# Attention decoding: the first part of the first keys in two loads of 64 partitions each instead of one of 128

## The chip, the cores and the metric

The kernel runs on one core of a Trainium2 chip. The metric is the device time of one execution in microseconds, the median of the runs. A profile of one execution, taken by the hardware profiler, is read beside it; its span goes from the first to the last instruction and is a little shorter than the measured time.

## What is computed

Attention for one query position against 65,536 keys, with 32 query heads that share 8 key and value heads (four to one). All tensors are bfloat16; D is 128.

```python
B, Hq, Hkv, Sq, Sk, D = 1, 32, 8, 1, 65536, 128
...
k = jnp.repeat(k, rep, axis=1)
v = jnp.repeat(v, rep, axis=1)
scale = D ** -0.5
scores = jnp.einsum("bhqd,bhkd->bhqk", q, k) * scale
p = _softmax(scores, axis=-1)
return jnp.einsum("bhqk,bhkd->bhqd", p, v)
```

The keys and the values are 134.2 MB each, and each byte is read from HBM once.

## The kernel before

**Tiling.** A head's 65,536 keys are taken in two rounds of 32,768 (`NR` is 16 rounds in all for the 8 heads, `HALVES` is 2). In a round each of the 128 partitions holds 2T = 256 consecutive keys of 128 numbers: 64 KB in a row, 8.39 MB over all partitions. A "row tile" is one key of each partition, 128 x 128 numbers. The keys of a round lie in `kbuf`, which has room for 256 + 96 row tiles, so that rounds alternate between two overlapping places; the values lie in `vbuf`, 256 row tiles.

**A round.** TensorE transposes the key tiles in groups of TB = 8 into one of four PSUM buffers (`pe_transposes`, line 139); VectorE and ScalarE copy them to `ktb` in SBUF (`evict`, lines 233 and 235); TensorE multiplies each with the four queries of the head (`pe_scores`, line 157), LAG = 8 groups behind the transposes. The maximum over a part of the scores is taken on VectorE and GpSimd, the exponentials on ScalarE (line 403), and TensorE multiplies them with the values (`stretch`, line 183). A round is cut into 160 and 96 row tiles (A and C), each with its own maximum.

**Loads.** All loads of keys and values are issued by SyncE (SP) in `sync_engine`, in the order in which they stand there, on one queue. A key load waits for `kfree`, which ScalarE raises (line 231) when the first 160 row tiles of the round before are transposed; a value load waits for `vfree`. From the second head on, each round is one load of keys and one of values of 8.39 MB. The loads of the first head and of the last rounds are cut into parts, so that work can start sooner at the beginning and little is left to do at the end. The keys of round 0 come in three parts, at `K_PARTS` = (0, 64, 160): 64, 96 and 96 row tiles of all 128 partitions, or 2048, 3072 and 3072 KB. They go to the columns C to C + 256 of `kbuf`.

**Semaphores.** Each part of the keys has one, `krdy[0]` to `krdy[2]`. A load adds 16 to it when it has landed. TensorE waits for `krdy[n]` and takes the 16 away again (`take`, lines 42 to 45) ahead of the group of transposes that needs the part: `krdy[0]` before group 0, `krdy[1]` before group 8, and `krdy[2]` before group 19. Such waits stand in the profile under line 45, the line of `take`.

**The start.** TensorE waits for the queries and an identity matrix, transposes the queries (line 215), waits for their copy (`t_qT`) and enters the loop over the rounds, whose beginning is aligned with up to 16 empty instructions. The first thing in the loop is the wait for `krdy[0]`.

Of the kernel before, what the change touches and what calls it, by code (L numbers as in the profile page):

```python
# [10 lines left out]
P = 128  # L11
# [3 lines left out]
C = 96  # L15
A = 2 * T - C
K_PARTS = (0, 64, A)
# [24 lines left out]
def take(e, sem, n=1):  # L42

    e.wait_ge(sem, n)
    e.sem_inc(sem, -n)  # L45


def bass_standalone__gqa_softmax__decode_kernel(nc, q, k, v, out):
# [14 lines left out]
    def row_tile(odd, x):  # L63
        return (x + C) % (2 * T) if odd else x
# [6 lines left out]
    def sb(name, shape, dt):  # L71
        return S(nc.sbuf_tensor(name, shape, dt))

    def sem(name):
        return S(nc.semaphore(name))

    kbuf = sb("kbuf", [P, (2 * T + C) * D], DT.bfloat16)
# [38 lines left out]
    krdy = [sem(f"krdy{i}") for i in range(len(K_PARTS))]  # L116
    vrdy = [sem(f"vrdy{i}") for i in range(2)]
    vpiece = [sem(f"vpiece{i}") for i in range(len(V_PIECES))]
    kfree, vfree, vmid = sem("kfree"), sem("vfree"), sem("vmid")
    trd, tra, evd, eva = sem("trd"), sem("tra"), sem("evd"), sem("eva")  # L120
    qkd, qrdy, pvd = sem("qkd"), sem("qrdy"), sem("pvd")
# [42 lines left out]
    def pe_keys(pe, i):  # L164
        for j in range(GA + LAG):
            if j < GA:
                pe_transposes(pe, j, C + j * TB)
            if j >= LAG:
                pe_scores(pe, j - LAG)
        with pe.If(i % 2 > 0):  # L170
            for j in range(GA, G):
                pe_transposes(pe, j, j * TB - A)
        with pe.If(i % 2 < 1):
            for j in range(GA, G):
                pe_transposes(pe, j, C + j * TB)
        for j in range(GA, G):
            pe_scores(pe, j)
# [11 lines left out]
    def pe_values(pe, i):  # L189

        take(pe, vrdy[0], 16)
        take(pe, exd)
        stretch(pe, 1).then_inc(vmid, 1)


        with pe.Fori(i % 2, 2) as s:
            with pe.If(s > 0):
                take(pe, vrdy[1], 16)  # L200
                take(pe, exd)
                stretch(pe, 2).then_inc(pvd, 1)
            with pe.If((i + s) % 2 < 1):
                take(pe, exd)
                stretch(pe, 0).then_inc(pvd, 1)

    def pe_last(pe):
        ins = pe.transpose(fin[0:R, 0:P], acc, identf[:, :])  # L208
        ins.wait_op(t_acc, 1, "sem-ge")
        ins.then_inc(s_fin, 1)  # L210

    def tensor_engine(pe):
        pe.wait_ge(q_sem, 16)
        pe.wait_ge(t_id, 1)
        pe.transpose(trb[0][:, 0:HR], qsb[:, :], ident[0:HR, 0:HR]).then_inc(s_x, 1)
        pe.wait_ge(t_qT, 1)
        pe.addr_align(256, offset=LOOP_SLOT, max_nops=16)
        with pe.Fori(0, NR) as i:
            pe_keys(pe, i)
            pe_values(pe, i)  # L220
        pe_last(pe)
# [221 lines left out]
    def pairs(x):  # L443

        return x.rearrange("h (c p t) d -> (h c) p (t d)", c=HALVES, p=P)

    def sync_engine(e):
        kp, vp = pairs(kf), pairs(vf)

        def cols(a, b):  # L450
            return slice(a * D, b * D)

        def load_k(i, odd, split=(0,)):

            for n, f in enumerate(split):
                last = (split + (len(K_PARTS),))[n + 1]
                a, b = K_PARTS[f], (K_PARTS + (2 * T,))[last]
                r = row_tile(odd, a) if b - a < 2 * T else 0
                t = r if odd else C + r
                e.dma_start(kbuf[:, cols(t, t + b - a)], kp[i][:, cols(r, r + b - a)]).then_inc(krdy[f], 16)  # L460
                for x in range(f + 1, last):
                    e.sem_inc(krdy[x], 16)

        def load_v(i, ready, a, b):
            e.dma_start(vbuf[:, cols(a, b)], vp[i][:, cols(a, b)]).then_inc(ready, 16)

        def load_both(i, odd):
            take(e, kfree)
            load_k(i, odd)
            take(e, vfree)  # L470
            load_v(i, vrdy[0], 0, 2 * T)
            e.sem_inc(vrdy[1], 16)

        load_k(0, 0, (0, 1, 2))
        load_v(0, vrdy[0], 0, 2 * T)

        for sm in [vrdy[1]] + vpiece:
            e.sem_inc(sm, 16)

        take(e, kfree)  # L480
        load_k(1, 1)
        e.wait_ge(vmid, 1)
        load_v(1, vrdy[0], C, A)
        take(e, vfree)
        e.sem_inc(vpiece[0], -16)
        load_v(1, vrdy[1], A, 2 * T)
        load_v(1, vpiece[0], 0, C)
        with e.Fori(1, H - 1) as h:
            load_both(2 * h, 0)
            load_both(2 * h + 1, 1)  # L490
        i = NR - 2
        take(e, kfree)
        load_k(i, 0, (0, 2))
        take(e, vfree)
        load_v(i, vrdy[0], 0, A)
        load_v(i, vrdy[1], A, 2 * T)
        i = NR - 1
        take(e, kfree)
        load_k(i, 1, (0, 1, 2))
        take(e, vfree)  # L500
        for sm in vpiece:
            e.sem_inc(sm, -16)
        load_v(i, vrdy[0], C, 2 * T)
        e.sem_inc(vrdy[1], 16)
        r = 0
        for n, sm in zip(V_PIECES, vpiece):
            load_v(i, sm, r, r + n)
            r += n
        ins = e.dma_start(of[HR - R:HR, :], olast[:, :])
        ins.wait_op(t_last, 1, "sem-ge")  # L510
        ins.then_inc(o_sem, 16)
        e.wait_ge(o_sem, 32)

    block = S(nc.Block())
    block.tensor(tensor_engine)
    block.vector(vector_engine)
    block.scalar(scalar_engine)
    block.gpsimd(gpsimd_engine)
    block.sync(sync_engine)
    es.close()  # L520

# [26 lines left out]
```

## Time and profile before

| | |
|---|---|
| median of 3 runs | 629.46 us (629.41 to 629.58) |
| the profiled execution's own time | 629.4 us |
| its span | 627.5 us |
| mean granted TensorE clock | 0.767 |
| busy: TensorE / VectorE / ScalarE / GpSimd | 489.5 / 284.5 / 235.4 / 16.4 us |
| moved by DMA | 268.59 MB, mean 428 GB/s |

How to read it: times are microseconds from the span's start unless ns stands beside them. PE is TensorE, PEld its weight loads, DVE VectorE, ACT ScalarE, POOL GpSimd; SPq and PEq are the instruction queues of SyncE and TensorE, which issue transfers and wait for semaphores. L139 is line 139 of the kernel. "x64" is a count of instructions. What stands in square brackets is the idle time of the engine before the instruction, and what ended it.

### The profile page before, as it was taken

The page shows a single profiled execution, that of the slowest core. Times are in us where ns is not written, and L with a number is a line of the kernel's source. Part 1 is how long each engine was busy: PE and PEld are TensorE (multiplying, and loading weights), DVE is VectorE, ACT ScalarE, POOL GpSimd, SP SyncE. Part 2 cuts the span into 40 slices and gives each one's busy share as a digit, 9 for nine tenths or more (in the row PEclk, how much of TensorE's full clock was granted, in tenths as well). Part 3 has the DMA queues.
Part 4 walks back from the last instruction along what each step waited for, and adds up shares of the span by engine and source line. Part 5 has one row for each costly group of instructions (what it writes and reads, how often), then busy time and mean ns, then how long its engine had stood idle before and what let it go on. Part 6 is the DMA issues. An engine that isn't in the chain of part 4 may idle for free. (4 is left out here: it accounts for less than half of the span.)

```text
span 627.5 us, 26947 instructions
## 1 busy us (share of the span) xinstructions
PE 489.5 (78%) x12290; PEld 484.9 (77%) x12290; DVE 284.5 (45%) x667; ACT 235.4 (38%) x466; POOL 16.4 (3%) x49
## 2 busy tenths in 40 slices
PE   4764995949859597694977949679695894999987
PEld 4664995949859597694977949679695894999886
DVE  4340553616436164451644517245172542747364
ACT  2240442605425154350533605235152451535343
POOL 0000000000000000000000000000000000000000
PEclk9775886959768597795977959678596885969697
DMA  9999999999999999999999999999999999999997
GB/s 378 427 450 402 439 453 418 451 418 451 418 451 418 447 422 439 430 426 439 426 439 430 434 434 430 439 430 439 430 434 434 434 434 430 415 436 429 425 438 303
DMA packets 6443, 268.59 MB, mean 428 GB/s; under 512 B 802, under 2 KB 930, under 8 KB 1186
## 3 DMA queue, kind: packets, MB, share of 16 engines
q1 hardware_dynamic: 6344, 268.44, 99.2%
q8 instruction: 7, 0.11, 0.1%
q10 hardware_dynamic: 90, 0.02, 0.0%
q14 instruction: 2, 0.02, 0.0%
HBM read 268.44 MB, written 0.01 MB: 428 GB/s over the span
## 5 line engine op out<-in xcount | busy, mean ns | idle before, releaser
L139 PE MATMUL trb<-ident,kbuf 128*128 128x128 bf16 x4096 | 302.2, 237 | 108.6 <-PEq L45 102.8
L139 PEld LDWEIGHTS trb<-ident,kbuf 128*128 128x128 bf16 x4096 | 269.9, 107 | 110.3 <-issue 108.0
L233 ACT ACTIVATE ktb<-trb 128x1024 bf16<-128x1024 bf16 x176 | 180.2, 1024 | 350.2 <-PE trb L139 343.7
L235 DVE COPY ktb<-trb 128x1024 bf16<-128x1024 bf16 x336 | 221.7, 688 | 170.2 <-PE trb L139 167.0
L157 PE MATMUL qkb<-qcur,ktb 128*128 128x4 bf16 x4096 | 132.4, 164 | 0.7 <-issue 0.7
L157 PEld LDWEIGHTS qkb<-qcur,ktb 128*128 128x128 bf16 x4096 | 124.6, 96 | 0.8 <-issue 0.8
L183 PE MATMUL pvb<-pts,vbuf 128*128 128x4 bf16 x2560 | 71.7, 166 | 13.4 <-PEq L45 10.0
L183 PEld LDWEIGHTS pvb<-pts,vbuf 128*128 128x128 bf16 x2560 | 69.9, 102 | 15.2 <-issue 14.9
L403 ACT ACTIVATE pts<-qkb,negm 128x160 bf16<-128x160 f32 (+1 forms) x128 | 52.0, 549 | 0.0
L183 PE MATMUL qkb<-pts,vbuf 128*128 128x4 bf16 x1536 | 43.4, 166 | 8.1 <-PEq L45 8.1
L183 PEld LDWEIGHTS qkb<-pts,vbuf 128*128 128x128 bf16 x1536 | 42.4, 104 | 8.7 <-issue 8.6
L270 DVE TENSOR_REDUCE cmax<-qkb 128x4 f32<-128x640 f32 (+1 forms) x32 | 22.1, 691 | 59.0 <-DVEq L45 59.0
L403 ACT ACTIVATION_READ_ACCUMULATOR pts<-qkb,negm 128x1 f32 x128 | 34.2, 268 | 0.0
L439 POOL PARTITION_ALL_REDUCE cmaxa<-cmax x32 | 12.0, 375 | 576.3 <-POOLq L45 576.3
L320 DVE COPY acc<-qkb 128x4 f32<-128x4 f32 x8 | 1.3, 162 | 41.3 <-DVEq L45 41.3
L397 ACT ACTIVATE alpha<-dm 128x4 f32<-128x4 f32 x32 | 6.4, 201 | 32.1 <-ACTq L45 32.1
L298 DVE TENSOR_TENSOR lp<-lp,alpha 128x4 f32<-128x4 f32 x24 | 3.9, 163 | 26.9 <-DVEq L45 26.9
L309 DVE TENSOR_TENSOR acc<-acc,pvb 128x4 f32<-128x4 f32 x32 | 5.0, 157 | 21.0 <-DVEq L45 20.2
L287 DVE TENSOR_TENSOR m<-m,cmaxa 128x4 f32<-128x4 f32 x24 | 3.8, 159 | 8.8 <-DVEq L45 8.8
L306 DVE TENSOR_TENSOR acc<-acc,alpha 128x4 f32<-128x4 f32 x24 | 3.9, 162 | 4.2 <-DVEq L45 3.7
L288 DVE TENSOR_TENSOR dm<-m 128x4 f32<-128x4 f32 x24 | 3.9, 162 | 0.8
L299 DVE TENSOR_TENSOR lp<-lp,rsum 128x4 f32<-128x4 f32 x24 | 3.9, 161 | 0.8
(42 smaller groups left out, 30.1 us busy)
## 6 DMA issues: line engine op xcount, KB each, us to landing
kbuf<-in_k_dram SPq DMA_DIRECT2D x5, 3072.0 KB, 24.2
vbuf<-in_v_dram SPq DMA_DIRECT2D x2, 5120.0 KB, 23.2
vbuf<-in_v_dram SPq DMA_DIRECT2D x3, 3072.0 KB, 19.6
kbuf<-in_k_dram SPq DMA_DIRECT2D x1, 5120.0 KB, 17.4
kbuf<-in_k_dram SPq DMA_DIRECT2D x2, 2048.0 KB, 12.6
vbuf<-in_v_dram SPq DMA_DIRECT2D x1, 2048.0 KB, 18.0
vbuf<-in_v_dram SPq DMA_DIRECT2D x1, 1984.0 KB, 30.9
vbuf<-in_v_dram SPq DMA_DIRECT2D x1, 704.0 KB, 32.2
```

The lines of the kernel that those rows point to most:

```text
L139: ins = pe.transpose(trb[j % NTB][:, i * P:(i + 1) * P], kbuf[:, t * D:(t + 1) * D], ident[:, :])
L157: ins = pe.matmul(bank[:, t * R:(t + 1) * R], lhsT=ktb[:, off:off + P], rhs=qcur[:, :], start=True, stop=True)
L183: ins = pe.matmul(vsum[q], lhsT=vbuf[:, r * D:(r + 1) * D], rhs=pts[:, r * R:(r + 1) * R], start=r == a, stop=r == b - 1)
L233: ins = e.activation(dst, trb[j % NTB][:, :], AF.Copy).then_inc(eva, 1)
L235: ins = e.tensor_copy(dst, trb[j % NTB][:, :]).then_inc(evd, 1)
L270: e.tensor_reduce(cmax[:, :], qkb[part][:, 0:n * R].rearrange("p (t g) -> p g t", g=R), AX.X, ALU.max).then_inc(cm, 1)
L288: lambda: e.tensor_tensor(dm[u % 2][:, :], mo[:, :], mn[:, :], ALU.subtract),
L298: chain(e, lambda: e.tensor_tensor(lp[:, :], lp[:, :], alpha[u % 2][:, :], ALU.mult), lambda: e.tensor_tensor(lp[:, :], lp[:, :], rsum[u % ...
L309: return lambda: e.tensor_tensor(acc, acc, vsum[q], ALU.add)
L397: e.activation(alpha[u % 2][:, :], dm[u % 2][:, :], AF.Exp, scale=scale)
L403: ins = e.activation(pv[:, g, r:r + n], sv[:, g, 0:n], AF.Exp, bias=negm[b][:, g:g + 1], scale=scale, accum_out=rsum[b][:, g:g + 1])
L439: e.partition_all_reduce(cmaxa[:, :], cmax[:, :], P, bass.bass_isa.ReduceOp.max).then_inc(cma, 1)
```

## The change

The first part of the keys of round 0 (64 row tiles, `kbuf` columns C to C + 64) was one load of 128 partitions that signalled `krdy[0]`. It is now two loads, issued one after the other on the same queue in the same place: partitions 0 to 63, which signal a new semaphore `kfirst`, and partitions 64 to 127, which signal `krdy[0]`. Each moves 64 rows of 16 KB. TensorE waits once for `kfirst` ahead of its loop, and in the loop for `krdy[0]` as before. The two other parts of round 0 are issued by the same function as before, `load_k`, now called for the parts 1 and 2 alone. No other load and no other instruction is changed.

```diff
+    kfirst = sem("kfirst")
...
         pe.wait_ge(t_qT, 1)
+        pe.wait_ge(kfirst, 16)
         pe.addr_align(256, offset=LOOP_SLOT, max_nops=16)
...
-        load_k(0, 0, (0, 1, 2))
+
+        n = K_PARTS[1]
+        for p, sm in ((0, kfirst), (P // 2, krdy[0])):
+            e.dma_start(kbuf[p:p + P // 2, cols(C, C + n)],
+                        kp[0][p:p + P // 2, cols(0, n)]).then_inc(sm, 16)
+        load_k(0, 0, (1, 2))
         load_v(0, vrdy[0], 0, 2 * T)
```

## The prediction

> **What bounds the kernel now.** I read the page's 40 slices and its queue list first, to see which resource is busy from end to end.
>
> ```profile
> DMA  9999999999999999999999999999999999999997
> ...
> q1 hardware_dynamic: 6344, 268.44, 99.2%
> ...
> PE 489.5 (78%) x12290; PEld 484.9 (77%) x12290; DVE 284.5 (45%) x667; ACT 235.4 (38%) x466; POOL 16.4 (3%) x49
> ```
>
> The 16 DMA engines are at 90% or more in 39 of 40 slices. One queue, SP's, carries 268.44 MB (all of k and v, each byte once), and its packets fill 99.2% of the span. No compute engine is above 78%. So I went on to the rate of the transfers, stage by stage. In the view of busy times by window the last two columns are the mean DMA share and GB/s; a packet counts in the window in which it starts.
>
> ```profile
> core 0: us, PE busy (x) PEld busy (x) DVE busy (x) ACT busy (x) POOL busy (x), PEclk, DMA share, GB/s
> 0.00:1.60 1.60, 0.00 (x0) 0.00 (x0) 0.50 (x6) 0.41 (x1) 0.93 (x9) 1.00 0.00 0
> 1.60:2.80 1.20, 0.00 (x0) 0.00 (x0) 0.74 (x5) 1.08 (x2) 0.05 (x1) 1.00 0.93 219
> 2.80:7.60 4.80, 0.20 (x1) 0.10 (x1) 1.88 (x13) 0.00 (x0) 0.00 (x0) 1.00 1.10 466
> 7.60:15.00 7.40, 6.51 (x64) 6.37 (x64) 3.46 (x5) 2.42 (x3) 0.00 (x0) 1.00 0.98 421
> 15.00:100.00 85.00, 58.58 (x1472) 57.83 (x1472) 31.95 (x75) 26.82 (x56) 1.94 (x5) 0.71 1.01 432
> 100.00:200.00 100.00, 80.43 (x1921) 79.99 (x1922) 47.27 (x99) 38.46 (x67) 2.30 (x6) 0.76 1.00 433
> ...
> 400.00:500.00 100.00, 75.77 (x1841) 75.30 (x1839) 43.73 (x99) 34.78 (x64) 1.98 (x6) 0.73 1.00 433
> 500.00:600.00 100.00, 86.46 (x2208) 85.62 (x2206) 49.00 (x111) 41.61 (x86) 2.67 (x7) 0.80 1.00 430
> 600.00:624.00 24.00, 21.79 (x634) 21.56 (x632) 14.06 (x41) 11.34 (x26) 1.19 (x3) 0.88 0.97 411
> 624.00:627.50 3.50, 1.24 (x29) 0.82 (x26) 0.50 (x2) 0.00 (x0) 0.00 (x0) 0.50 0.01 2
> ```
>
> Nothing moves before 1.6 us, and almost nothing after 624. Between them the rate is about 433 GB/s at a share of 1.00, window after window: 268.44 MB at 433 GB/s is 620.0 us of the 622.4 between. The stream has no hole that could swallow a delay. The end is the start of the first byte, plus the bytes over the rate, plus a tail of 3.5 us. The second question is who waits for the first bytes.
>
> ```profile
> 0.73 1.36 SPq L460 DMA_DIRECT2D kbuf<-in_k_dram  x3
> 2.14 0.59 SPq L465 DMA_DIRECT2D vbuf<-in_v_dram  x1
> 26.02 0.33 SPq L460 DMA_DIRECT2D kbuf<-in_k_dram  x1
> ...
> 4.92 0.20 PE L215 MATMUL trb<-ident,qsb 32*128 32x32 bf16 x1 [4.92 <-DMA qsb<-in_q_dram]
> 8.07 6.51 PE L139 MATMUL trb<-ident,kbuf 128*128 128x128 bf16 x64 [2.95 <-PEq L45]
> 16.88 0.61 PE L139 MATMUL trb<-ident,kbuf 128*128 128x128 bf16 x8 [2.29 <-PEq L45]
> ...
> kbuf<-in_k_dram SPq DMA_DIRECT2D x1, 2048.0 KB, 7.2
> ...
> PE trb L139 <- PEq L45: 102.8, 18, 9.0
> ```
>
> The first key load (2048 KB) is issued at 0.73 us and lands 7.2 us later, at 7.9; the first transposes start at 8.07, after an idle 2.95 us. TensorE then eats its 64 row tiles by 14.6 and waits again, 2.29 us, for the second part. In all it stands 102.8 us, 18 times, at line 45, the wait-and-subtract on a semaphore, before transposes, for keys above all. So TensorE follows the stream from the first part on.
>
> **The change, part by part.** *Removed:* one load of 128 partitions x 16 KB (64 row tiles x 128 x 2 bytes), 2.097 MB. *Added:* two loads of 64 partitions x 16 KB, partitions 0 to 63 and then 64 to 127, 1.049 MB each, on the same queue; one semaphore, and one wait of TensorE for it ahead of the loop. The bytes and the 128 rows of 16 KB are the same.
>
> *The rate of half the partitions* is the one large term, and the trace of before has no load of k or v that writes fewer than 128 partitions. Its bounds:
> - From below: the halves run as fast as the whole. The 2.097 MB take 2.097/0.433 = 4.84 us as now, and the cost is 0. The row for it is the same 433 GB/s, if the limit lies in the 16 engines and not in where they write.
> - From above: each half of the partitions takes at most what it takes now. 433 GB/s into 128 partitions is 216.5 into 64; no row shows a half taking more. Each load then needs 1.049/0.2165 = 4.84 us, the two in turn 9.69, and the cost is 4.84 us.
>
> I take the upper one, for two reasons. It is the only rate that the rows show for one half of the partitions, and the lower one needs twice that. And the rate is nearly the same with rows of 16 KB, of 24 KB (421 GB/s from 7.6 to 15 us, with the 3072 KB parts) and of 64 KB (433 later), which speaks for a fixed width of a path rather than for something that a transfer's shape can speed up.
>
> [...]
>
> *The issue on SP.* Three key issues take 1.36 us, 0.45 each; a fourth puts the value load's issue from 2.14 to about 2.6. Cost 0: the engines still have the first part to move until 7.6 us and two 3072 KB parts behind it. If that cover were gone, it would cost 0.45. In the other direction, the first load has half the rows to describe and its bytes might start sooner: issue at 0.73, first bytes after 1.6, so a gain below 0.87 us. I take 0 for both: the start is the same instruction at the same place, and the nearest row, the first window with bytes, gives no split of those 0.87 us.
>
> *The wait on TensorE.* Behind it stand the padding of the loop, the loop's entry, the old wait for the first part, and all transposes. The second half is the later one, so the old wait still ends last; the new one is over by then and is covered by the 2.95 us that TensorE idles there. Without that cover it would be one more semaphore wait, once. DVE and ACT wait for the first transposes, as now. Nothing else is moved: the other two key parts, the value load and every later load keep their order.
>
> *Where the delay goes.* The first part lands 4.84 us later, at 12.8 instead of 7.9, and the 64 transposes start at about 12.9. The second and third part and the values stand in the same queue and come 4.84 us later too. The key buffer is freed as late, so the issue at 26.02 comes near 30.9; the queue still holds most of the values then, so the stream stays as full as now, only shifted. What hides part of it? Nothing that I find: the share is about 1.00 in each long window.
>
> ```profile
> kbuf<-in_k_dram SPq DMA_DIRECT2D x13, 24.9
> ...
> vbuf<-in_v_dram SPq DMA_DIRECT2D x13, 27.1
> ```
>
> A whole key or value load of 8.39 MB needs 19.4 us at 433 GB/s, and lands 24.9 or 27.1 after its issue: some 5.5 to 7.7 us of earlier bytes are still queued when it is issued, and they will be after the change, since issue and landing shift together.
>
> *Sum.* Profiled execution 629.4 us (span 627.5, and 1.9 around it), plus 4.84 for the halves, 0 for issue, wait and moves: **634.2 us**, span 632.3. The median of the runs is 629.46, so the profiled one is typical.
>
> **The rivals.**
>
> *A: the halves run at full rate.* The limit is in the engines, or each half is served by engines of its own, so that both flow at once. For it: the share of 1.00 is a share of engine time, so a limit of the engines would look the same. Against it: it needs 433 GB/s into 64 partitions, or a division of the work that the rows don't show. This is the way that ends on the other side, not slower: the only term left is the start of the first bytes, worth up to 0.87 us if the smaller load is described faster, against up to 0.45 for the additional issue. Time 628.5 to 629.9, most likely 629.4; it decides as soon as a half takes more than about 340 GB/s (the cost, 4.84 x (433/rate - 1), is then below 1.3 us). That the change does nothing looks the same.
>
> *B: the halves overlap in part.* Engines that get through their share of the first half early turn to the second while others still write the first. For it: they don't start in step; 219 GB/s in 1.6 to 2.8 us against 466 after it shows a ragged start of about half of 1.2 us. Against it: 0.6 us of raggedness is little beside 4.84 per half. If half of the loss is won back: 629.4 + 2.4 = 631.8 us, with all between 630.7 and 633.5 counted here.
>
> *C: the second half waits for the landing of the first,* as well as running at half rate. Issue to landing is 7.2 us for 4.84 of moving, so 2.4 more: 636.6 us. Against it: between the first and second part, around 7.6 us, the rate doesn't break off (466, then 421 GB/s).
>
> **How the numbers follow.** The forecast (half rate, 634.2, own range 633.5 to 634.9) gets 0.69, A 0.17, B 0.08, C 0.03. The last 0.03 are for a gain of over 0.2% (1.26 us, about what a measurement of this kernel tells from no change), for which I find no mechanism: the whole idle start is 1.6 us, and the part that the change can touch is 0.87. So faster 0.03, same 0.17, slower 0.69 + 0.08 + 0.03 = 0.80. The unknown term reaches from 0 to 4.84, so the range has to hold both ends: from 629.2 (A's cluster, for the most part) to 635.3 (the forecast, with 0.45 for an uncovered issue and 0.6 for raggedness). C and the lowest of A are left out.
>
> **What the new profile would show.** In the windows: about 217 GB/s from 1.6 to 11 us, where there are 466 now, and 433 from about 12.5 on. If A holds, 433 stands there from the start. The first transposes start near 12.9 us with about 7.8 us of idle before them (B: near 10.5; A: 8.1), the second issue of whole keys near 30.9, and the last window with traffic ends near 629 in place of 624. DMA engines would look as busy as before in the slices, since their packets only take longer: twice as long in the first part. The prediction is wrong if the first transposes move by 4 us or more and the end does not: then the stream has a reserve that I don't see, most likely at its last loads. It is also wrong if the first part lands on time and the end still moves, which would put the cost on the queue behind it.

## The result, and the profile after

| | before | after |
|---|---|---|
| median of the runs | 629.46 us (629.41 to 629.58, 6 runs) | 634.77 us (634.63 to 634.81, 6 runs) |
| the profiled execution's own time | 629.4 us | 634.79 us |
| its span | 627.5 us | 632.7 us |

The changed kernel takes 1.0084 times as long (95% interval 1.0074 to 1.0094), 5.31 us more; the forecast was 634.2 us.

The view of busy times by window, of the kernel after, with nearly the windows that the prediction shows (the last two columns are the DMA share and GB/s):

```profile
core 0: us, PE busy (x) PEld busy (x) DVE busy (x) ACT busy (x) POOL busy (x), PEclk, DMA share, GB/s
1.60:2.80 1.20, 0.00 (x0) 0.00 (x0) 0.74 (x5) 1.05 (x2) 0.05 (x1) 1.00 0.78 198
2.80:7.60 4.80, 0.18 (x1) 0.10 (x1) 1.87 (x13) 0.00 (x0) 0.00 (x0) 1.00 1.03 225
7.60:12.00 4.40, 0.00 (x0) 0.00 (x0) 0.00 (x0) 0.00 (x0) 0.00 (x0) 1.00 1.01 218
12.00:15.00 3.00, 1.56 (x16) 1.59 (x17) 0.51 (x1) 0.00 (x0) 0.00 (x0) 1.00 0.94 374
15.00:100.00 85.00, 63.16 (x1523) 62.23 (x1521) 34.13 (x76) 29.22 (x58) 1.94 (x5) 0.74 1.01 435
...
624.00:629.00 5.00, 5.00 (x181) 4.89 (x179) 2.25 (x14) 1.54 (x9) 0.43 (x1) 0.50 0.83 337
629.00:632.70 3.70, 1.46 (x35) 1.00 (x33) 0.98 (x6) 0.00 (x0) 0.00 (x0) 0.50 0.03 7
```

From 2.8 to 12 us the queue moves 218 to 225 GB/s, where it moved 466 and 421 before. From 15 us on it is back at its old rate (435 GB/s up to 100 us, 432 before). The DMA share is about 1.00 in both stretches (1.03 and 1.01 after, 1.10 and 0.98 before): it is the time in which packets are under way, and at half the bytes and the same share they took twice as long. Who looks at the share alone sees no change.

Both columns count a packet whole, in the window in which it starts, so that in a short window both can be too high or too low together. GB/s divided by the share beside it is steadier: 218 and 216 GB/s at a full share for the two windows after, 424 and 430 for 466 and 421 before.

The timeline of the kernel after, SyncE's queue and TensorE (start, duration, instruction, and the idle time before it):

```profile
0.73 1.20 SPq L479 DMA_DIRECT2D kbuf<-in_k_dram  x2
1.98 1.13 SPq L462 DMA_DIRECT2D kbuf<-in_k_dram  x2
31.03 0.33 SPq L462 DMA_DIRECT2D kbuf<-in_k_dram  x1
...
13.44 6.31 PE L140 MATMUL trb<-ident,kbuf 128*128 128x128 bf16 x64 [9.85 <-PEq L45]
21.86 0.64 PE L140 MATMUL trb<-ident,kbuf 128*128 128x128 bf16 x8 [2.10 <-PEq L45]
```

The first transposes start 5.4 us later (13.44 for 8.07), those of the second part 5.0 us later (21.86 for 16.88), the load of the next round's keys is issued 5.0 us later (31.03 for 26.02), and the end comes 5.3 us later. Nothing catches up on the way. The list of waits has the same 18 waits of TensorE before transposes, 12 us longer in total than before, 6.9 of them in the first wait (9.85 for 2.95):

```profile
PE trb L140 <- PEq L45: 114.8, 18, 9.8
```

### The profile page after: what moved, and what is told of

Its sections match the earlier page's. It is cut to its first block, busy times and chain, and to the rows that moved or that the text cites. A ratio compares the mean times of both kernels' runs of the same rounds, so it can differ in the third digit from the quotient of the medians.

```text
span 632.7 us, 26949 instructions
## 1 busy us (share of the span) xinstructions
PE 485.8 (77%) x12290; PEld 481.1 (76%) x12290; DVE 283.8 (45%) x667; ACT 235.2 (37%) x466; POOL 16.4 (3%) x49
## 5 line engine op out<-in xcount | busy, mean ns | idle before, releaser
L140 PE MATMUL trb<-ident,kbuf 128*128 128x128 bf16 x4096 | 298.4, 235 | 120.7 <-PEq L45 114.8
L140 PEld LDWEIGHTS trb<-ident,kbuf 128*128 128x128 bf16 x4096 | 266.1, 106 | 122.5 <-issue 119.9
L184 PEld LDWEIGHTS pvb<-pts,vbuf 128*128 128x128 bf16 x2560 | 69.9, 102 | 13.7 <-issue 13.4
```

The lines of the kernel that those rows point to most:

```text
L140: ins = pe.transpose(trb[j % NTB][:, i * P:(i + 1) * P], kbuf[:, t * D:(t + 1) * D], ident[:, :])
L184: ins = pe.matmul(vsum[q], lhsT=vbuf[:, r * D:(r + 1) * D], rhs=pts[:, r * R:(r + 1) * R], start=r == a, stop=r == b - 1)
```

## Experiments

The theory: of the 433 GB/s that go into 128 partitions, 0 to 63 can take one half and 64 to 127 the other, and the engines take the two loads in turn, so that half of the rate goes unused. The expectations speak of paths that the partitions share; that is the author's supposition, and what the runs show is the rate of each load. Its rivals: a cost of each additional or smaller load; a limit of each partition or of any 64-partition load; a cost that lies at the start only. The kernel before stands at 629.44 us in the first four experiments and at 629.37 in the second four. The first six edits are of the kernel after, the last two of the kernel before; "..." stands for lines left out.

### Two loads, cut by row tiles instead of partitions

```diff
-        for p, sm in ((0, kfirst), (P // 2, krdy[0])):
-            e.dma_start(kbuf[p:p + P // 2, cols(C, C + n)],
-                        kp[0][p:p + P // 2, cols(0, n)]).then_inc(sm, 16)
+        for c, sm in ((0, kfirst), (n // 2, krdy[0])):
+            e.dma_start(kbuf[:, cols(C + c, C + c + n // 2)],
+                        kp[0][:, cols(c, c + n // 2)]).then_inc(sm, 16)
```

> The first part in two loads of all 128 partitions x 32 row tiles (8 KB rows), the same two semaphores and the same additional issue as the change. If the cost of the change is the rate of half the partitions: no loss but the start, 629.3 to 629.9 us, first transposes near 8.1 to 8.5 us. If the cost is that of a second, smaller load on the queue (its issue, its completion, 1 MB in place of 2): 633 to 635 us, as with the change.

Measured: 629.63 us (629.55 to 629.85), ratio to before 1.0003 (0.9993 to 1.0012). Its windows:

```profile
2.80:7.60 4.80, 0.20 (x1) 0.10 (x1) 1.88 (x13) 0.00 (x0) 0.00 (x0) 1.00 1.12 474
7.60:12.00 4.40, 3.78 (x39) 3.81 (x40) 1.57 (x3) 1.02 (x1) 0.00 (x0) 1.00 0.94 400
```

The same bytes in two loads of 1 MB, with the same two waits, run at the full rate: 423 and 426 GB/s, divided by the share. The additional load, issue, semaphore and wait cost nothing that can be measured (629.63 us for 629.44); the cut by partitions does.

### The two halves on two queues

```diff
+        n, p = K_PARTS[1], P // 2
+        e.dma_start(kbuf[0:p, C * D:(C + n) * D],
+                    pairs(kf)[0][0:p, 0:n * D]).then_inc(kfirst, 16)
         e.dma_start(qsb[:, :], qf).then_inc(q_sem, 16)
...
-        for p, sm in ((0, kfirst), (P // 2, krdy[0])):
-            e.dma_start(kbuf[p:p + P // 2, cols(C, C + n)],
-                        kp[0][p:p + P // 2, cols(0, n)]).then_inc(sm, 16)
+        p = P // 2
+        e.dma_start(kbuf[p:P, cols(C, C + n)], kp[0][p:P, cols(0, n)]).then_inc(krdy[0], 16)
```

> The same two halves of 64 partitions, but issued on two queues: partitions 64 to 127 from SP as before, partitions 0 to 63 from ScalarE's queue, ahead of the queries. If the cost is that the engines write one half after the other, and they alternate between the two queues row by row: both halves are written at once, 629.4 to 630.5 us, first transposes near 8.5. If they empty one queue's load before the other, or if a 64-partition load as such is slow: 634.3 to 635.3 us, first transposes near 13.4.

Measured: 634.74 us (634.5 to 634.8). The two issues and the first transposes in the timeline, the landings in the list of issues (KB each, us from issue to landing), the one queue that moved keys in the first 4 us (q10 is ScalarE's, q1 SyncE's; packets, MB, share), and the windows:

```profile
0.73 0.57 SPq L482 DMA_DIRECT2D kbuf<-in_k_dram  x1
0.73 0.56 ACTq L421 DMA_DIRECT2D kbuf<-in_k_dram  x1
...
14.77 6.50 PE L140 MATMUL trb<-ident,kbuf 128*128 128x128 bf16 x64 [1.39 <-PEq L45]
```

```profile
kbuf<-in_k_dram SPq DMA_DIRECT2D x1, 1024.0 KB, 12.6
kbuf<-in_k_dram ACTq DMA_DIRECT2D x1, 1024.0 KB, 8.9
```

```profile
q10 hardware_dynamic: 33, 0.54, 57.1%
```

```profile
2.80:7.60 4.80, 0.00 (x0) 0.00 (x0) 1.28 (x9) 0.64 (x2) 0.00 (x0) 1.00 1.00 222
7.60:12.00 4.40, 0.00 (x0) 0.00 (x0) 0.00 (x0) 0.00 (x0) 0.00 (x0) 1.00 1.07 235
```

Both halves are issued at 0.73 us, but ScalarE's lands 3.7 us ahead of SyncE's, in the first 4 us only ScalarE's queue moves keys, 0.54 of its 1.05 MB, and the rate stays at half (222 and 220 GB/s, divided by the share): the engines didn't alternate between the two queues from the start. Two queues don't make two halves flow together here. The first transposes start at 14.77 us and not near 13.4, because the queries stand behind the keys on ScalarE's queue and land only near 13 us (11.8 us after their issue at 1.32); the end doesn't move with them (634.74 us for the change's 634.77), so it is the stream that it follows. By itself this run can't tell the theory from a slow 64-partition load; the next three can.

### Four loads of 32 partitions, eight of 16

```diff
-        for p, sm in ((0, kfirst), (P // 2, krdy[0])):
-            e.dma_start(kbuf[p:p + P // 2, cols(C, C + n)],
-                        kp[0][p:p + P // 2, cols(0, n)]).then_inc(sm, 16)
+        w = 32
+        for p in range(0, P, w):
+            e.dma_start(kbuf[p:p + w, cols(C, C + n)],
+                        kp[0][p:p + w, cols(0, n)]).then_inc(krdy[0] if p + w == P else kfirst, 16)
```

The wait for `kfirst` is for 48 here. With w = 16 it is for 112.

> The first part in four loads of 32 partitions each, in order. If half of the partitions shares half of the paths, and 32 neighbouring partitions reach as many of them as 64 do: 217 GB/s again, first part 9.7 us, total 634.5 to 635.5 us. If each partition has a limit of its own (433/128 = 3.4 GB/s): 108 GB/s, 19.4 us for the part, 14.5 more than before, near 644.3 us. If the rate does not depend on partitions but each additional load costs what the change cost: three additional loads, 3 x 5.3, near 645.4 us, first transposes near 24. [...]

> The first part in eight loads of 16 partitions each, in order. If 16 neighbouring partitions reach half of the paths that 32 or 64 reach: 108 GB/s, 19.4 us for the part, near 644.3 us, first transposes near 23. If any load below 128 partitions gets half the rate, whatever its partitions: near 635 us. If each partition has a limit of its own: 54 GB/s, 38.7 us, near 663.6 us. If each additional load costs 5.3 us: 7 x 5.3, near 666.6 us.

Measured: 634.41 us (634.31 to 634.68) with 32, and 641.21 us (640.99 to 641.57) with 16. Windows of the first, then of the second:

```profile
2.80:7.60 4.80, 0.20 (x1) 0.10 (x1) 1.87 (x13) 0.00 (x0) 0.00 (x0) 1.00 1.01 220
```

```profile
2.80:7.60 4.80, 0.20 (x1) 0.10 (x1) 1.88 (x13) 0.00 (x0) 0.00 (x0) 1.00 1.13 138
7.60:12.00 4.40, 0.00 (x0) 0.00 (x0) 0.00 (x0) 0.00 (x0) 0.00 (x0) 1.00 1.03 127
12.00:15.00 3.00, 0.00 (x0) 0.00 (x0) 0.00 (x0) 0.00 (x0) 0.00 (x0) 1.00 0.98 120
```

The loads of 32 partitions get what those of 64 get, 220 GB/s (218 divided by the share), and four such loads cost no more than two of 64 (634.41 us for 634.77); the time is 0.1 us below the range expected for this. So the limit is not one of each partition, and additional loads are not what costs. With 16 the rate falls again, to 120 to 138 GB/s (122 or 123 in each window, divided by its share). The expectation, which supposed for 16 partitions half of what 32 get, gave 108, and 644.3 us; measured are 11.8 us more than before in place of 14.8. That some engines are already at the next 16 partitions while others finish would explain the difference, if those have a rate of their own, and would fit the interleaved loads below; it is an argument only, and no trace shows it.

### The 64 partitions in the middle

```diff
-        for p, sm in ((0, kfirst), (P // 2, krdy[0])):
-            e.dma_start(kbuf[p:p + P // 2, cols(C, C + n)],
-                        kp[0][p:p + P // 2, cols(0, n)]).then_inc(sm, 16)
+        for p, w in ((32, 64), (0, 32), (96, 32)):
+            e.dma_start(kbuf[p:p + w, cols(C, C + n)],
+                        kp[0][p:p + w, cols(0, n)]).then_inc(krdy[0] if p == 96 else kfirst, 16)
```

The wait for `kfirst` is for 32.

> The first part in three loads: partitions 32 to 95 (64 of them, 1 MB), then 0 to 31, then 96 to 127 (0.5 MB each). If the limit is in paths of which partitions 0 to 63 share one half and 64 to 127 the other, the load of 32 to 95 reaches both halves and runs at the full rate, and only the other 1 MB at half: 2.42 us more for it and 0.3 for the later start, 632.2 us; 433 GB/s from 2 to 4.5 us. If any load of 64 partitions gets half the rate, or each partition has a limit: 634.4 to 635.0 us, 217 GB/s from the start. If three loads cost more than two as such: above 635.

Measured: 632.56 us (632.39 to 632.84), ratio 1.0051 (1.0035 to 1.0068). The landing of its first load:

```profile
kbuf<-in_k_dram SPq DMA_DIRECT2D x1, 1024.0 KB, 5.7
```

and its windows; by 5 us about 1.0 MB has started, nearly the size of the first load:

```profile
2.80:5.00 2.20, 0.18 (x1) 0.10 (x1) 1.71 (x13) 0.00 (x0) 0.00 (x0) 1.00 0.81 343
5.00:8.00 3.00, 0.00 (x0) 0.00 (x0) 0.17 (x1) 0.00 (x0) 0.00 (x0) 1.00 1.05 268
```

This run decides between how many partitions and which. A load of 64 partitions, of the same 1 MB and the same 16 KB rows, lands 5.7 us after its issue when the partitions are 32 to 95; the first load of the kernel after, partitions 0 to 63, has this row:

```profile
kbuf<-in_k_dram SPq DMA_DIRECT2D x1, 1024.0 KB, 7.7
```

The 343 GB/s at a share of 0.81 are 423 GB/s at a full share, the rate of a whole load (424 to 430 before). The sum of the theory, half of the loss for half of the bytes, gave 632.2. For a load of 64 partitions it matters which they are: 423 GB/s for 32 to 95, 216 to 218 for the lower and the upper half. That any 64 neighbouring rows of the keys are slow to read is excluded too, since this load reads 64 such rows, as the halves do. One thing these runs can't separate: in each of them partition p is filled from row p of the source, so a limit that divides the rows read in just this way, and not the partitions written, would look the same.

### Small pieces, lower and upper half in turn

```diff
-        for p, sm in ((0, kfirst), (P // 2, krdy[0])):
-            e.dma_start(kbuf[p:p + P // 2, cols(C, C + n)],
-                        kp[0][p:p + P // 2, cols(0, n)]).then_inc(sm, 16)
+        w = 16
+        for c in range(0, n, w):
+            for p in (0, P // 2):
+                e.dma_start(kbuf[p:p + P // 2, cols(C + c, C + c + w)],
+                            kp[0][p:p + P // 2, cols(c, c + w)]).then_inc(
+                                krdy[0] if p and c + w == n else kfirst, 16)
```

The wait for `kfirst` is for 112.

> The first part in eight loads of 64 partitions x 16 row tiles (4 KB rows, 256 KB), lower half and upper half in turn. If the cost is that all engines write one half at a time, then with pieces of 0.6 us, less than the 1.2 us by which the engines lie apart at the end of a load in the runs so far, some write the upper half while others write the lower: 630 to 633 us. If they stay in step: 634.5 to 635 us. If each additional load of half the partitions has a cost of its own: well above 635.

Measured: 633.49 us (633.29 to 633.56). Its issues in the timeline, and a window:

```profile
0.73 5.04 SPq L481 DMA_DIRECT2D kbuf<-in_k_dram  x8
```

```profile
5.00:8.00 3.00, 0.00 (x0) 0.00 (x0) 0.17 (x1) 0.00 (x0) 0.00 (x0) 1.00 1.02 242
```

Eight loads of half the partitions cost 1.3 us less than two, and the rate is 242 GB/s in place of 218 to 225 (237 in place of 216 to 218, divided by the share). That fits a loss by turns, with engines that lie on both halves part of the time, though the trace doesn't show which half an engine writes. They overlap less than expected: the time is 0.5 us above the 630 to 633. The issues don't hold the pieces up: 256 KB in 0.63 us each are 416 GB/s, more than is moved.

### More bytes in halves: the second part, and the next round's keys

In the first of these two, part 0 is whole again and part 1 (96 row tiles) is in halves; both add to `krdy[1]`, and TensorE waits for 32 there. In the other, the keys of round 1 are in halves that both add to `krdy[0]`, which is waited for with 32.

The other loads that use the same semaphore raise it by 16 more in each case, so that the count of 32 holds in every round.

```diff
-                take(pe, krdy[n], 16)
+                take(pe, krdy[n], 32 if n == 1 else 16)
...
-        load_k(0, 0, (0, 1, 2))
+        a, b = K_PARTS[1:3]
+        e.dma_start(kbuf[:, cols(C, C + a)], kp[0][:, cols(0, a)]).then_inc(krdy[0], 16)
+        for p in (0, P // 2):
+            e.dma_start(kbuf[p:p + P // 2, cols(C + a, C + b)],
+                        kp[0][p:p + P // 2, cols(a, b)]).then_inc(krdy[1], 16)
+        load_k(0, 0, (2,))
```

```diff
-                take(pe, krdy[n], 16)
+                take(pe, krdy[n], 32 if n == 0 else 16)
...
-        load_k(1, 1)
+        for p in (0, P // 2):
+            e.dma_start(kbuf[p:p + P // 2, cols(0, 2 * T)],
+                        kp[1][p:p + P // 2, cols(0, 2 * T)]).then_inc(krdy[0], 16)
+        for x in (1, 2):
+            e.sem_inc(krdy[x], 16)
```

> The first part whole again (128 partitions); the second part, 96 row tiles or 3.146 MB, in two halves of 64 partitions. If the cost is the rate of half the partitions, it grows with the bytes: 3.146 MB at 216.5 instead of 433 GB/s, 7.27 us more, 636.7 us; and the first bytes, now those of a whole load, start at the old time. If 0.5 us of the change's 5.3 belongs to each halved load and not to the start: 637.2 us. If the cost is a fixed one for a halved load: near 634.7 us.

> The keys of round 1 (8.389 MB, one load before) in two halves of 64 partitions, in the middle of the stream; all of round 0 as before the change. If the stream has no reserve: 8.389 MB at 216.5 instead of 433 GB/s, 19.4 us more, 648.8 us. If the 5.5 to 7.7 us of bytes that stand queued when a load is issued can swallow a delay: 641 to 643.5 us. If only a delay at the start counts, since nothing is ready before it: 629.5 us.

Measured: 637.89 us (637.65 to 638.09) and 652.50 us (652.11 to 652.99), 8.5 and 23.1 us more than before. Windows of the first:

```profile
8.00:10.00 2.00, 1.20 (x12) 1.23 (x13) 0.15 (x1) 0.00 (x0) 0.00 (x0) 1.00 0.96 197
10.00:12.60 2.60, 2.60 (x28) 2.60 (x26) 1.42 (x3) 1.02 (x1) 0.00 (x0) 1.00 1.01 205
12.60:20.00 7.40, 2.54 (x30) 2.36 (x28) 1.81 (x3) 2.05 (x2) 0.00 (x0) 0.85 1.01 213
```

and of the second, with SyncE's queue between 81 and 85 us (packets, MB, share) behind them:

```profile
42.00:50.00 8.00, 1.46 (x50) 1.43 (x51) 1.49 (x7) 1.54 (x9) 0.37 (x1) 0.54 0.81 166
50.00:60.00 10.00, 1.04 (x39) 0.98 (x37) 0.00 (x0) 0.00 (x0) 0.00 (x0) 0.50 1.03 212
60.00:70.00 10.00, 4.89 (x179) 4.75 (x175) 0.64 (x4) 0.00 (x0) 0.00 (x0) 0.50 1.02 211
70.00:80.00 10.00, 0.00 (x0) 0.00 (x0) 0.00 (x0) 0.00 (x0) 0.00 (x0) 0.50 1.02 210
80.00:84.00 4.00, 0.00 (x0) 0.00 (x0) 0.00 (x0) 0.00 (x0) 0.00 (x0) 0.50 0.52 107
...
q1 hardware_dynamic: 52, 0.59, 72.3%
```

The cost grows with the bytes, wherever in the stream they lie: 5.3, 8.5 and 23.1 us for 2.1, 3.1 and 8.4 MB. So it is neither a fixed one nor one of the start, and the bytes that stand queued when a load is issued swallow none of it.

Both are above the expected 7.3 and 19.4, since half the partitions get less than half of the rate here. Divided by its share, each window of the second run gives 205 to 207 GB/s, the first and the last too: their 166 and 107 stand beside low shares, since fewer packets happen to start in them; the three windows of the first give 203 to 211. At 206 GB/s the 3.146 MB take 15.3 us, 8.0 more than at 433, and the 8.389 MB 40.7 us, 21.4 more. Of the 1.7 us left in the second run, about 1.5 are in the value load behind the keys: its first 0.59 MB start between 81 and 85 us, while the last packets of the halves are under way, and move at 204 GB/s of a full share as well, though they go to all 128 partitions. The 0.5 us left in the first run are about what the change itself has beyond its sum (below).

## Why the prediction was right

**The bound** held: the stream goes on from the first byte to 3.7 us before the end (DMA shares of 0.94 to 1.03 from 2.8 to 624 us, 0.83 from there to 629), and a delay in it reaches the end whole. The experiment with the keys of round 1 shows it for the middle of the stream, where the prediction had only argued it.

**The rate of half the partitions**, the one large term, was taken at its upper bound, 4.84 us for 216.5 GB/s. The windows after show 218 to 225 (216 to 218 divided by the share), and the first transposes and all that follows come 5.0 to 5.4 us later. The reason given, a fixed width of a path, was the author's supposition: it fits the loads of 32 partitions (220 GB/s) and of the middle 64 (423), but no run shows a path itself, or that the limit lies where the partitions are written and not where their rows are read. The prediction could not know it: the equal rate for rows of 16, 24 and 64 KB fits a limit of the engines as well, and no row of before told the two apart.

**The issue and the start** were set to 0, with a gain of up to 0.87 us held possible. They went the other way. The two new issues take 1.20 us, 0.60 each where 0.45 was expected, the value load is issued at 3.15 us where 2.6 was, and the first bytes come some 0.3 us later. The windows before, then after (the 15 and 26 GB/s add up to the 8 KB of the queries):

```profile
1.60:1.80 0.20, 0.00 (x0) 0.00 (x0) 0.07 (x1) 0.20 (x1) 0.05 (x1) 1.00 1.41 328
1.80:2.00 0.20, 0.00 (x0) 0.00 (x0) 0.17 (x1) 0.20 (x1) 0.00 (x0) 1.00 2.33 492
```

```profile
1.60:1.80 0.20, 0.00 (x0) 0.00 (x0) 0.07 (x1) 0.20 (x1) 0.05 (x1) 1.00 0.07 15
1.80:2.00 0.20, 0.00 (x0) 0.00 (x0) 0.17 (x1) 0.20 (x1) 0.00 (x0) 1.00 0.14 26
2.00:2.20 0.20, 0.00 (x0) 0.00 (x0) 0.06 (x1) 0.20 (x1) 0.00 (x0) 1.00 2.08 492
```

**The sum** is 0.5 us short: 5.31 measured for 4.84. That is not the late start. SyncE's queue has moved this much in the first 300 us, before and after:

```profile
q1 hardware_dynamic: 2784, 128.98, 99.8%
...
q1 hardware_dynamic: 2768, 126.88, 99.7%
```

The 2.10 MB less are 4.85 us at 433 GB/s, with the late start in them, and in the first 600 us they are 2.08 MB. So the stream is late by what the sum says, and in this closeness is some luck. The start is late, and away from the seam between the two loads the rate is below 216.5, as these windows of the kernel after show (208 and 205 GB/s, divided by the share). Around the seam it is higher (220 from 7 to 8.5 us, 240 GB/s at a share of 1.09), so that the departures nearly cancel.

```profile
4.50:7.00 2.50, 0.00 (x0) 0.00 (x0) 0.48 (x4) 0.00 (x0) 0.00 (x0) 1.00 1.01 210
8.50:11.00 2.50, 0.00 (x0) 0.00 (x0) 0.00 (x0) 0.00 (x0) 0.00 (x0) 1.00 0.99 203
```

The missing 0.5 us come after that, in the last 30 us of the stream, in its tail or outside the span; what they are stays open. They are hardly more than the noise: the interval of the ratio, 1.0074 to 1.0094, is 4.7 to 5.9 us and holds the 4.84. The two loads cut by row tiles, which run at the full rate, take 0.2 us more than the kernel before as well.

**The wait on TensorE** cost nothing: the two loads cut by row tiles have it too and take 629.63 us. It was covered by the idle time before the first transposes, now 9.85 us. The forecast said 7.8; the queries came earlier in the profiled execution (1.6 us after their issue for 4.1), so TensorE was free sooner, which nothing waits for.

**The rivals.** A, the full rate, fell for the lower and upper half and is true for the middle 64 partitions (423 GB/s), which no row of before could tell. B, an overlap, seems real but small: 1.3 us with eight pieces, and with two only the higher rate at the seam. C, a wait for the landing, is excluded by the rate: the first half lands at 8.4 us (7.7 after its issue), and the windows on both sides of 7.6 us are full (shares of 1.03 and 1.01). The issue of the next keys at 31.03 us and the last traffic at 629 are where the forecast put them (30.9 and 629). The 5.5 to 7.7 us of queued bytes that it read from issue to landing are too many, since the first load has 2.4 us there besides its moving; the sum doesn't use them.

## What to carry to other kernels

Where the stream of transfers is the bound, load all 128 partitions at a time and cut a load by its columns if it has to come in parts: that cut cost nothing that could be measured here (629.63 us for 629.44), while the cut into a lower and an upper half ran at half the rate (216 to 218 GB/s for 424 to 430). If only 64 partitions are loaded, these runs speak for the middle (32 to 95 ran at 423 GB/s) rather than 0 to 63. Judge such a load by GB/s, not by how busy the DMA engines look: their share was 1.03 and 1.01 at half the rate.

## What the runs showed of the hardware that had not been expected

A load of 64 partitions took longer to issue than the first load of 128. In the run with the second part in halves, the whole first part's issue took 0.43 us and each half's 0.59:

```profile
0.73 0.43 SPq L477 DMA_DIRECT2D kbuf<-in_k_dram  x1
1.22 1.18 SPq L479 DMA_DIRECT2D kbuf<-in_k_dram  x2
```

The loads of 32 partitions took 0.45 us each, and those of 16 the same (eight in 3.64 us):

```profile
0.73 1.80 SPq L480 DMA_DIRECT2D kbuf<-in_k_dram  x4
```

In the middle of the stream the two halves of round 1's keys took 1.19 us, where the kernel before issues the whole load in 0.33.

So in these runs an issue doesn't grow with the number of partitions (0.45 us for 16 and 32, 0.56 to 0.63 for 64, 0.33 to 0.67 for 128), and why 64 are slow stays open. Loads of 128 are not always quick either: the value load of the kernel before took 0.59 us, and two key parts in the run with two queues 0.67 each. And of two loads that were issued at the same time on two queues, only one moved in the first 4 us, and they landed 3.7 us apart: the queues were not served row by row in turn from the start.
